# Reordering the head and the second layer norm's lead-in of a fused attention and MLP training kernel

## The chip, the cores and the metric

The kernel runs on one core of a Trainium2 chip. The metric is the device time of one execution in microseconds (us). The core has TensorE (PE, matmuls; PEld are its weight loads), VectorE (DVE), ScalarE (ACT) and GpSimd (POOL). Each of them runs its own instructions in the order in which the program lists them, and waits where one of them needs another engine's result. DMA transfers are issued by SyncE (SP) and POOL, and at some places by ACT. An issue that has to wait holds everything that is queued behind it on the same engine.

## The reference, cut to what matters

```python
h  = x + A(layernorm(x))            # x: 2048 x 640, bf16
#   A: q, k, v = x @ wqkv, 32 heads of 20
#      pq, pk = phi(q), phi(k);  phi(t) = where(t > 0, t + 1, exp(t)) + 1e-6
#      kv = pk^T v per head, z = sum of pk;  o = (pq kv) / (pq z + 1e-6);  A = o @ wo
h2 = h + B(layernorm(h))
#   B: (silu(x @ w1) * (x @ w3)) @ w2,  F = 1728
# outputs: h2 and the gradients for x, wqkv, wo, w1, w3, w2, given grad_out
```

## The kernel before, in words

The 2048 rows are 16 tiles of 128 (`t`), the 640 features 5 chunks of 128. The program is one straight list of instructions, written out by hand; nothing reorders it. `m_part` and its like accumulate in PSUM, for which a few named pairs of buffers ("big", "tr", "m", "mm", "at", "o2") are reused in turn.

**The head (lines 415 to 496).** The x tiles and the key weights (`load_wq(2, 3)` and `(3, 4)`, the two halves) are loaded first, then w2 and grad_out by transposing DMAs. While x tile 0 travels, TensorE runs 44 matmuls on ones. Each tile is normalized by `ln1`: `part` takes the statistics (L147, L150, L151) on VectorE, POOL raises the variance to the power -0.5 (L152), and `norm` subtracts the mean and multiplies (L155). The first eight tiles are transposed on TensorE (`p1_tr`, L249) and copied to `pqT` by ScalarE (L251); the others are transposed by DMA. Step `t` of the loop at L463 then holds, in this order: the key product of tile t in two halves of 320 columns (L255), for t < 3 the transposes of tile t + 1, the statistics of tile t + 4 and the norm of tile t + 3, `phi` (ScalarE's Exp and Relu, L272 and L273, and later VectorE's `rest`, L276 and L277), in some steps a q tile, for steps 2 to 5 a chunk of gradient @ w2^T (`ghh_chunk`, L364 with PSUM "gp") and the transposes of tile t + 2, and from step 3 on the products of pk and normalized x (`m_part`, L385, PSUM "macc"), which read tile t - 3. `trickle` names the steps that load pieces of w1, w3, the v weights and wo.

**After the loop (L498 to L558).** q tiles 4 to 9, the sums `Z` of pk (`z_late`) and their copy over all partitions (`z_row`, L322, L324), the denominators of the attention (`r_prod` on POOL, `r_red`, `r_inv`, `r_scale` on VectorE; `r_head` is the last three and a transposing DMA) and the first two blocks of `kvT` run beside the products of `m_part`. `mT` holds their transposes, by DMA for parts 0 to 3 (L397).

**Lead-in to the MLP (L780 to L790).** The list in `run` names the steps one by one: q tiles 10 to 15 (`q_late`, two halves each), `f2_kv` 2 to 4 (L404, and the masks on VectorE, L205, into `bd`), `f2_wT` 0 to 4 (L610, with a copy and a transposing DMA into `Wp`, L613, L614), then for tiles 0 to 4 the attention's output added to x (`f2_half`, L572, L577), the second layer norm (`f2_hn`) and its transposes (`f2_ht`, L663), with chunks 4 to 7 of gradient @ w2^T (`mlp_ghh`) between them.

**The MLP (L830 to L873).** Four blocks `c` of 512 rows, each with 14 chunks `fc` of F; the last chunk has 64 columns of w2 that are real and 64 of zeros. Chunks come in pairs. For each pair VectorE runs seven operations (`mlp_pair`, L727), three of them with a store to DRAM: `hh` from SP, `gate * gh` from SP and `gh` from POOL. ScalarE writes the next `gate` but one into the same buffer (L693). The second layer norm of the next block's tiles runs beside it.

Of the kernel before, what the change touches and what calls it, by code (L numbers as in the profile page):

```python
# [55 lines left out]
def kernel(  # L56
# [73 lines left out]
    class Stats:  # L130
# [12 lines left out]

        def part(self, src, t, j):
            if j == 0:
                self.st[t] = cp.tile([P, 2, 6], F32, name="st6", bufs=4)
            V.bn_stats(out=self.st[t][:, j, :], in_=src[:, t, j * HD:(j + 1) * HD])  # L147
            if j == 0:
                return
            V.bn_aggr(out=self.mv[:, t, :], in_=self.st.pop(t)[:])  # L150
            V.tensor_scalar(out=self.ve[:, t:t + 1], in0=self.mv[:, t, 1:2], scalar1=EPS_LN, scalar2=None, op0=ALU.add)  # L151
            G.tensor_tensor(out=self.rs[:, t:t + 1], in0=self.ve[:, t:t + 1], in1=mhalf[:, 0:1], op=ALU.pow)  # L152

        def norm(self, out, src, t):
# [24 lines left out]
    def load_x(a, b):  # L179
        dma(out=x_sb[:, a:b, :], in_=xS[:, a:b, :])  # L180

    load_x(1, 2)
    A.activation(sg[:], zero[:], AF.Exp)
    load_wq(2, 3)
    load_wq(3, 4)
    load_x(2, 3)
    load_x(3, 4)
# [44 lines left out]
    XT_DMA = 8  # L232
    WARM = 44

# [9 lines left out]
    def p1_tr(t, parts=((0, DT),)):  # L244
        xn = x_sb[:, t, :]
        for a, b in parts:
# [4 lines left out]
            A.copy(out=pqT[:, a:b, t * P:(t + 1) * P], in_=tr[:, a:b, :])  # L251

    def p1_half(acc, t, n0):
        for c in range(DT):
            T.matmul(acc, lhsT=pqT[:, c, t * P:(t + 1) * P], rhs=wqkv[:, c, n0:n0 + HD], start=(c == 0),  # L255
                     stop=(c == DT - 1))

    def p1_mm(t, n0):
        acc = ps.tile([P, 2, 512], F32, name="big", bufs=2)
        for j in range(2):  # L260
            p1_half(acc[:, j, 0:HD], t, n0 + j * HD)
        return acc

# [4 lines left out]

    def phi(acc, dst, then=None):

        mq, rq = (p1.tile([P, D], BF16, name=n, bufs=b) for n, b in (("mq", 3), ("rq", 3)))
        A.activation(two(mq[:]), acc[:, :, 0:HD], AF.Exp)  # L272
        A.activation(two(rq[:]), acc[:, :, 0:HD], AF.Relu)  # L273

        def rest():
            V.tensor_scalar(out=mq[:], in0=mq[:], scalar1=1.0, scalar2=1e-6, op0=ALU.min, op1=ALU.add)  # L276
            V.tensor_tensor(out=dst, in0=mq[:], in1=rq[:], op=ALU.add)  # L277
            if then is not None:
                then()
        held.append(rest)  # L280
# [18 lines left out]
    def q_tile(t):  # L299
        q_home(t)  # L300
        phi(p1_mm(t, 0), pqs[t])

# [65 lines left out]
    def ghh_chunk(n, acc):  # L368

        c, fc = divmod(n, FT)  # L370
        mm5_to(acc, w2T, fc, g2T[c])
        if n % 2 == 0:
            ghh[n // 2] = pf.tile([P, 2, W], BF16, name="ghh", bufs=4)
        A.copy(out=ghh[n // 2][:, n % 2, :], in_=acc[:])  # L374
# [41 lines left out]
    load_w2T(0, 2 * P)  # L416
    load_g2T(0)
    load_w2T(2 * P, 4 * P)
    load_x(8, 12)
    load_wq(0, 2)  # L420
    load_x(12, ST)
    warm = ps.tile([P, 512], F32, name="warm", tag="tr", bufs=2)
    for _ in range(WARM):
        T.matmul(warm[:, 0:P], lhsT=ones[:], rhs=ones[:], start=True, stop=True, skip_group_check=True)
    ln1.run(x_sb, 0, 1)
    ln1.part(x_sb, 1, 0)
    for a, b in ((0, 2 * P), (2 * P, D)):
        ln1.norm(x_sb[:, 0, a:b], x_sb[:, 0, a:b], 0)
    p1_tr(0, ((0, 2), (2, DT)))
    for t in (1, 2):  # L430
        if t == 1:
            ln1.part(x_sb, t, 1)
            p1_norm(t)
            ln1.run(x_sb, t + 1, t + 2)
        else:
            ln1.part(x_sb, t + 1, 0)
            p1_norm(t)
    ln1.part(x_sb, 3, 1)
    w13 = [go for c0, c1 in ((0, 2), (2, 4), (4, 5)) for go in load_w13(c0, c1)]
    w13 += [lambda: dma(out=w1[:, :, F:FP], in_=rows(B_w3)[:, :, F - FL:F])]  # L440

    def load_wo():
        dma(out=wo[:], in_=A_wo.rearrange("(c p) n -> p c n", p=P))

    trickle = {3: w13[0], 4: w13[1], 11: lambda: load_wq(4, 6), 12: w13[2], 14: w13[3], 15: load_wo}

    stat_of = {t: (t + 4,) for t in range(7)}
    stat_of.update({7: (11, 12), 8: (13,), 9: (14,), 10: (15,)})
    norm_of = {t: (t + 3,) for t in range(8)}
    norm_of.update({8: (11, 12), 9: (13,), 10: (14,), 11: (15,)})  # L450
# [8 lines left out]

    outs = {6: ((group_out, 0),), 7: ((xn_out, 0, dma),), 10: ((group_out, 1), (xn_out, 1, dma)), 13: ((group_out, 2),)}  # L460

    QT = (5, 7, 9, 11)
    for t in range(ST):  # L463
        k = p1_mm(t, D)
        if t < 3:
            p1_tr(t + 1, ((0, 2), (2, DT)))
        for n in stat_of.get(t, ()):
            ln1.run(x_sb, n, n + 1)
            if on_act(n):
                ln1.bias(n)  # L470
        for n in norm_of.get(t, ()):
            if not on_act(n):
                p1_norm(n)
        phi_rest(t < 4)
        phi(k, pk_all[:, t, :])
        for n in norm_of.get(t, ()):
            if on_act(n):
                p1_norm(n)
        if t in QT:
            q_tile(QT.index(t))  # L480
        if 2 <= t < 6:
            ghh_chunk(t - 2, ps.tile([P, 2, 512], F32, name="gp", tag="big", bufs=2)[:, 0])
            p1_tr(t + 2)
        if t >= 3:
# [6 lines left out]
        for f, *n in outs.get(t, ()):  # L491
            f(*n)
        if t in trickle:
            trickle[t]()
    phi_rest()
# [16 lines left out]
    m_end(1)  # L512
    for go in w13[4:]:
        go()
    z_late((2, 3, 4), big())
    m_part(2, range(8))
    z_row((0, 1), big())
    z_row((2, 3, 4), big())
    r_prod(0)
# [4 lines left out]
    r_head(0)  # L524
    load_w2T(4 * P, 8 * P)
    r_prod(2)
# [24 lines left out]
    q_tile(9)  # L551
    r_head(5)
    r_prod(7)
    phi_rest()
# [166 lines left out]
    def mlp_pair(c, k, sig, s2, gate, up, gh):  # L721
# [13 lines left out]
        op(s2, gate, s2)  # L735
        op(gate, gate, gh, to=gg_d, r0=F)
        op(s2, s2, sig, ALU.add)
# [38 lines left out]
    def run(*steps):  # L776
# [4 lines left out]
    pkx.append(p1.tile([P, DT + 6, D], BF16, name="pkx", tag="pk"))  # L781
    run((q_late, 10, f2_mT), (f2_kv, 2), (f2_kv, 3), (f2_kv, 4), (phi_rest,), (q_late, 11), (f2_wT, 0), (f2_wT, 1),
        (phi_rest,), (q_late, 12), (f2_wT, 2), (f2_wT, 3), (phi_rest,), (q_late, 13, lambda: f2_wT(4)),
        (r_red, 6), (r_inv, 6), (r_scale, 6), (load_x, 2, 4), (r_T, 6), (q_late, 14), (load_x, 4, 8), (load_g2T, 1), (r_store, 4, 6),
        (mlp_ghh, 4), (q_late, 15),
        (sig_table,), (f2_half, 0, 0), (f2_half, 1, 0), (f2_half, 0, 1), (f2_half, 1, 1), (f2_hn, 0), (mlp_ghh, 5),
        (f2_half, 2, 0), (f2_hn, 1), (f2_m_out,), (load_w2T, 8 * P, 10 * P), (f2_half, 2, 1),
        (f2_ht, 0), (mlp_ghh, 6), (f2_half, 3, 0), (f2_hn, 2), (f2_w_out,), (f2_ht, 1), (f2_half, 3, 1), (phi_rest, 2),
        (q_out, 10, 14), (f2_ht, 2), (f2_hn, 3), (mlp_ghh, 7), (load_w2T, 10 * P, F), (f2_half, 4, 0), (f2_ht, 3),
        (f2_half, 4, 1), (r4_out,), (r_red, 7), (r_inv, 7), (r_scale, 7), (r_T, 7), (r_store, 6, 8), (q_out, 8, 10))  # L790
    p1.release()
# [38 lines left out]
    for c in range(SC):  # L830
# [8 lines left out]
        for fc in range(FT):  # L839
# [15 lines left out]
            if c == 2 and fc == 3:  # L855
                dmaG(out=rows(kvT_d), in_=bd[:])
            if fc == 3 and 0 < c < SC - 1:
                load_g2T(c + 1)
# [565 lines left out]
```

## Time and profile before

| what | value |
|---|---|
| median of 10 runs | 832.96 us (830.97 to 835.29) |
| profiled execution, own time | 833.86 us |
| its span | 832.2 us |
| VectorE, ScalarE, POOL busy | 454.1, 319.8, 110.5 us |
| granted TensorE clock | 1.00 |
| head and loop | 0 to 54 us |
| after the loop, lead-in to the MLP | 54 to 104 us |
| MLP | 104 to 350 us |

The span runs from the first to the last instruction of one execution; its own time holds what lies around that too. The profile gives, for each instruction, its engine, line, operation, the tile that it writes and those that it reads (`out<-in`), its shape, its start and its length. Idle time of an engine is put down to what ended it. Ends of matmuls are modelled with the pipeline's depth, so gaps between matmuls are better read from their starts. Some matmul records are missing from the trace, about one every ten microseconds.

### The profile page before, as it was taken

How to read it: one execution, taken by the hardware profiler on the slowest of the kernel's cores; microseconds unless marked ns; L12 is line 12 of the kernel's file. 1: busy time of each engine (PE TensorE's matmuls, PEld its weight loads, DVE VectorE, ACT ScalarE, POOL GpSimd, SP SyncE). 2: the span in 40 equal slices, each digit the busy share in tenths (PEclk: the TensorE clock that was granted, in tenths of full speed). 3: DMA queues.
4: the chain of work that ended last, by engine and by line, in shares of the span. 5: the costliest groups of instructions: out<-in, count | busy, mean ns of one | idle time of the engine just before them, and what ended most of it. 6: DMA issues, size and time to landing. Idle time of an engine off the chain costs nothing.

```text
span 832.2 us, 14209 instructions
## 1 busy us (share of the span) xinstructions
PE 818.8 (98%) x5540; PEld 522.8 (63%) x5568; DVE 454.1 (55%) x960; ACT 319.8 (38%) x605; POOL 110.5 (13%) x160
## 2 busy tenths in 40 slices
PE   8999999999999999999999999999999999999998
PEld 5676644555555555777777777777776777555554
DVE  6859787899898656400057777771680445200000
ACT  5855777655555666011121221222211433211111
POOL 2335222122121100000001111110220000000000
PEclk9999999999999999999999999999999999999999
DMA  9799998686574465999767888245998788886771
GB/s 258 206 310 186 215 309 252 219 212 169 143 203 142 129 204 166 211 255 269 218 153 186 185 217 202 62 110 105 237 216 168 172 192 177 212 197 138 164 168 37
DMA packets 323315, 157.59 MB, mean 189 GB/s; under 512 B 235312, under 2 KB 318160, under 8 KB 323248
## 3 DMA queue, kind: packets, MB, share of 16 engines
q1 hardware_dynamic: 293696, 127.73, 64.7%
q0 software_dynamic: 5136, 17.73, 6.5%
q10 hardware_dynamic: 24416, 11.23, 5.9%
q8 instruction: 43, 0.70, 0.4%
q14 instruction: 24, 0.20, 0.1%
HBM read 48.15 MB, written 51.46 MB: 120 GB/s over the span
## 4 chain that ended last, share of the span: by engine, by line
PE 82%; SPq 4%; DMA 1%; ACT 1%; DVE 0%; issue 0%; ACTq 0%
PE mm L364 20%; PE job L1189 17%; PE ghn L991 14%; PE gxn L1348 8%; PE o L751 7%; PE gw L944 7%; PE gwo L1076 3%; PE gr L1048 3%; SPq L1316 2%; PE at L572 2%; SPq L1153 1%; DMA gg_d<-gate 1%; SPq L1099 1%; PE dkv L1292 1%; PE dkv L1221 0%
## 5 line engine op out<-in xcount | busy, mean ns | idle before, releaser
L1189 PE MATMUL job<-gb,hnN 128*128 128x432 bf16 x640 | 117.0, 346 | 0.0
L991 PEld LDWEIGHTS <-ggb 128*128 128x128 bf16 x864 | 84.5, 98 | 32.8
L1189 PEld LDWEIGHTS <-hnN 128*128 128x128 bf16 x640 | 62.6, 98 | 54.1
L364 PE MATMUL mm<-pqT,w 128*128 128x512 bf16 x398 | 93.1, 379 | 0.6
L364 PEld LDWEIGHTS <-w 128*128 128x128 bf16 x540 | 52.8, 98 | 63.4 <-issue 0.3
L1193 ACT CAST obs<-job 128x432 bf16<-128x432 f32 (+1 forms) x60 | 29.2, 487 | 123.1 <-PE job L1189 123.1
L751 PE MATMUL o<-w,hhT 128*128 128x320 bf16 x448 | 67.5, 299 | 0.1
L991 PE MATMUL ghn<-w13a,ggb 128*128 128x320 bf16 x448 | 63.5, 299 | 0.0
L364 PE MATMUL mm<-g2T,w2T 128*128 128x512 bf16 x245 | 62.8, 379 | 0.6
L991 PE MATMUL ghn<-w13b,ggb 128*128 128x320 bf16 x416 | 61.4, 299 | 0.0
L751 PEld LDWEIGHTS <-hhT 128*128 128x128 bf16 x448 | 43.8, 98 | 23.6
L944 PE MATMUL gw<-g,hb 128*128 128x320 bf16 x416 | 57.0, 299 | 0.0
L374 ACT CAST ghh<-mm 128x512 bf16<-128x512 f32 x52 | 30.6, 588 | 55.0 <-PE mm L364 50.0
L944 PEld LDWEIGHTS <-hb 128*128 128x128 bf16 x416 | 40.6, 98 | 15.7
L1348 PE MATMUL gxn<-wqT,gT 128*128 128x320 bf16 x320 | 48.9, 299 | 1.1 <-DMA gT<-g_k 1.0
L1056 POOL TENSOR_TENSOR sz<-Zb,g_h 128x640 f32<-128x640 bf16 x16 | 20.2, 1262 | 199.4 <-DVE g_h L1054 107.7
L691 ACT ACTIVATE sig<-mm 128x512 bf16<-128x512 f32 x56 | 33.6, 599 | 28.3 <-PE mm L364 24.9
L364 PEld LDWEIGHTS <-w2T 128*128 128x128 bf16 x280 | 27.2, 98 | 27.1 <-issue 2.1
L255 PE MATMUL big<-wqkv,pqT 128*128 128x320 bf16 x260 | 39.5, 299 | 2.1 <-ACT pqT L251 0.6
L1003 ACT ACTIVATE gs<-ghn 128x640 bf16<-128x640 f32 x16 | 11.3, 704 | 78.6 <-PE ghn L991 73.7
L255 PEld LDWEIGHTS <-pqT 128*128 128x128 bf16 x320 | 30.6, 97 | 15.5 <-issue 2.2
L1348 PEld LDWEIGHTS <-gT 128*128 128x128 bf16 x320 | 31.1, 98 | 14.0 <-DMA gT<-g_k 1.3
(196 smaller groups left out, 1251.3 us busy)
## 6 DMA issues: line engine op xcount, KB each, us to landing
hh_d<-hhT SPq DMA_DIRECT2D x24, 256.0 KB, 2.6
gg_d<-gate SPq DMA_DIRECT2D x24, 256.0 KB, 3.4
gg_d<-ghh POOLq DMA_DIRECT2D x24, 256.0 KB, 3.4
ggb<-gg_d SPq DMA_DIRECT2D x6, 896.0 KB, 5.7
ggb<-gg_d SPq DMA_DIRECT2D x6, 832.0 KB, 6.1
out_dram<-obs ACTq DMA_DIRECT2D x40, 108.0 KB, 2.7
x_sb<-in_A_x_dram SPq DMA_DIRECT2D x6, 640.0 KB, 6.5
ggb<-gg_d SPq DMA_DIRECT2D x2, 1728.0 KB, 12.5
```

The source lines that it names most:

```text
L255: T.matmul(acc, lhsT=pqT[:, c, t * P:(t + 1) * P], rhs=wqkv[:, c, n0:n0 + HD], start=(c == 0), stop=(c == DT - 1))
L364: T.matmul(acc[:], lhsT=w[:, c, fc * P:(fc + 1) * P], rhs=rhs[:, c, :], start=(c == 0), stop=(c == DT - 1))
L374: A.copy(out=ghh[n // 2][:, n % 2, :], in_=acc[:])
L691: A.activation(sig[:, i, :], gp[:], AF.Sigmoid)
L751: T.matmul(o2["ps"][:, 0:HD], lhsT=hhT[c][:, fc, i * P:(i + 1) * P], rhs=w2[:, fc, j * HD:(j + 1) * HD], start=(fc == 0), stop=(fc == FT - 1))
L944: T.matmul(acc[:, j, 0:HD], lhsT=hb[b][:, t, i * P:(i + 1) * P], rhs=g2[:, t, j * HD:(j + 1) * HD], start=(t == 0), stop=(t == ST - 1))
L991: T.matmul(acc[:, j, 0:HD], lhsT=ggb[t // 2][:, k, lo:lo + P], rhs=rhs[:, j * HD:(j + 1) * HD], start=(k == 0), stop=(k == NG - 1))
L1048: T.matmul(gr[t][:, j, 0:HD], lhsT=ghT[t][:, c, :], rhs=wT2[:, c, j * HD:(j + 1) * HD], start=(c == 0), stop=(c == DT - 1))
L1076: T.matmul(acc[m][:, j, 0:n], lhsT=r_sb[:, t, m * P:(m + 1) * P], rhs=g_hx[:, t, j * HD:j * HD + n], start=(t == 0), stop=(t == ST - 1))
L1189: T.matmul(acc[:, 0:n], lhsT=lhs[:, t, m * P:(m + 1) * P], rhs=rhs(t), start=(t == 0), stop=(t == ST - 1))
L1193: A.copy(out=ob, in_=acc[:, 0:n])
L1348: T.matmul(acc[:, j, 0:HD], lhsT=g, rhs=wqT[:, k, j * HD:(j + 1) * HD], start=(k == 0), stop=(k == 14))
```

## The change

- x tile 2 is loaded between the halves of the key weights, x tiles 8 to 11 ahead of the second part of w2; 36 warm-up matmuls for 44.
- Tile 0 is only centred before it is transposed. Its key and q products get the scale in `phi`; the tile itself is multiplied in step 3 (`p1_scale`), after VectorE's `rest` of that step.
- The transposes of tiles 1 to 7 lie between the two halves of the previous tile's key product, in one piece; the gp chunks move from steps 2 to 5 to steps 3 to 6; the norms of tiles 2 and 3 come ahead of the loop.
- w1 and w3 are loaded in ten pieces and a tail instead of six and a tail, ten of the pieces inside the loop; the v weights are loaded in step 12, the second group of stores moves to step 11, and w2's rows 512 to 1023 are loaded ahead of `z_late`.
- Both `z_row` products use one PSUM buffer.
- `r_head(5)` and `r_prod(7)` move behind the last `f2_wT`; kv blocks and `f2_wT` lie between halves of q tiles; gp chunks 6 and 7 move between the transposes of the second layer norm; some stores and loads of the list move with them.
- The store of `gate * gh` is issued from POOL. The second block of grad_out is loaded in chunk 6 of block 0.
- The last chunk of w2 of each block: its 64 real columns are used twice, each time for 256 of the 512 rows, into PSUM partitions 0 to 63 and 64 to 127; POOL fills the rest of `gh` with zeros.

```diff
         def part(self, src, t, j, mid=None):
...
             V.bn_aggr(out=self.mv[:, t, :], in_=self.st.pop(t)[:])
+            if mid is not None:
+                mid()
...
+        def center(self, out, src, t):
+            V.tensor_scalar(out=out, in0=src, scalar1=self.mv[:, t, 0:1], scalar2=None, op0=ALU.subtract)
...
     load_wq(2, 3)
+    load_x(2, 3)
     load_wq(3, 4)
-    load_x(2, 3)
...
-    WARM = 44
+    WARM = 36
+    RAW = 1
...
+    def p1_scale(t):
+        xn = x_sb[:, t, :]
+        V.tensor_scalar(out=xn, in0=xn, scalar1=ln1.rs[:, t:t + 1], scalar2=None, op0=ALU.mult)
...
-    def p1_mm(t, n0):
+    def p1_mm(t, n0, between=None):
         acc = ps.tile([P, 2, 512], F32, name="big", bufs=2)
         for j in range(2):
             p1_half(acc[:, j, 0:HD], t, n0 + j * HD)
+            if j == 0 and between is not None:
+                between()
...
+        kw = dict(scale=ln1.rs[:, t:t + 1]) if t < RAW else {}
+        A.activation(two(mq[:]), acc[:, :, 0:HD], AF.Exp, **kw)
+        A.activation(two(rq[:]), acc[:, :, 0:HD], AF.Relu, **kw)
...
+        if fc == FT - 1:
+            gh, hw = ghh[n // 2], W // 2
+            G.memset(gh[FL:, 1, :], 0.0)
+            for d in range(DT):
+                for h in range(2):
+                    T.matmul(acc[h * FL:(h + 1) * FL, 0:hw], lhsT=w2T[:, d, fc * P:fc * P + FL],
+                             rhs=g2T[c][:, d, h * hw:(h + 1) * hw], start=(d == 0), stop=(d == DT - 1))
+            for h in range(2):
+                A.copy(out=gh[:FL, 1, h * hw:(h + 1) * hw], in_=acc[h * FL:(h + 1) * FL, 0:hw])
+            return
...
+    load_x(8, 12)
     load_w2T(2 * P, 4 * P)
-    load_x(8, 12)
...
+    ln1.part(x_sb, 0, 0)
+    ln1.part(x_sb, 0, 1, lambda: (center(0, 0, 2 * P), center(0, 2 * P, D)))
+    p1_tr(0, ((0, 2), (2, DT)))
     ln1.part(x_sb, 1, 0)
...
     for t in (1, 2):
+        ln1.part(x_sb, t, 1)
+        ln1.part(x_sb, t + 1, 0)
+        p1_norm(t)
     ln1.part(x_sb, 3, 1)
+    p1_norm(3)
+    w13 = [go for c in range(DT) for go in load_w13(c, c + 1)]
...
+    trickle = {3: w13[0:2], 4: w13[2:4], 9: w13[4:5], 10: w13[5:7], 12: (w13[7], load_vw), 14: w13[8:10], 15: (load_wo,)}
...
-        k = p1_mm(t, D)
-        if t < 3:
-            p1_tr(t + 1, ((0, 2), (2, DT)))
+        k = p1_mm(t, D, (lambda: p1_tr(t + 1)) if t + 1 < XT_DMA else None)
...
         phi_rest(t < 4)
+        if t == 3:
+            p1_scale(0)
...
-        if 2 <= t < 6:
-            ghh_chunk(t - 2, ps.tile([P, 2, 512], F32, name="gp", tag="big", bufs=2)[:, 0])
-            p1_tr(t + 2)
+        if 3 <= t < 7:
+            ghh_chunk(t - 3, ps.tile([P, 2, 512], F32, name="gp", tag="big", bufs=2)[:, 0])
...
-    for go in w13[4:]:
-        go()
+    w13[10]()
+    load_w2T(4 * P, 8 * P)
     z_late((2, 3, 4), big())
     m_part(2, range(8))
-    z_row((0, 1), big())
-    z_row((2, 3, 4), big())
+    zr = ps.tile([P, 2, 512], F32, name="bigx", tag="big", bufs=2)
+    z_row((0, 1), zr[:, 0])
+    z_row((2, 3, 4), zr[:, 1])
...
-    r_head(5)
-    r_prod(7)
...
-        op(gate, gate, gh, to=gg_d, r0=F)
+        op(gate, gate, gh, to=gg_d, r0=F, q=dmaG)
...
+    run((q_late, 10, f2_mT), (q_late, 11, kv3), (phi_rest,), (r_store, 4, 5),
+        (q_late, 12, lambda: (f2_wT(0), f2_wT(1))), (q_late, 13, lambda: (f2_wT(2), f2_wT(3))), (phi_rest,),
+        (q_late, 14, lambda: f2_wT(4)), (load_x, 2, 4), (r_head, 5), (r_prod, 7), (r_red, 6), (r_inv, 6), (f2_m_out,), (f2_w_out,),
+        (load_x, 4, 8), (q_out, 10, 14), (r_store, 5, 6), (load_w2T, 8 * P, 10 * P), (mlp_ghh, 4), (q_late, 15),
...
+        (f2_half, 2, 0), (f2_hn, 1), (load_w2T, 10 * P, F), (f2_half, 2, 1),
+        (f2_ht, 0), (f2_half, 3, 0), (f2_hn, 2), (f2_half, 3, 1), (mlp_ghh, 6), (f2_ht, 1), (mlp_ghh, 7), (f2_ht, 2),
+        (f2_hn, 3), (f2_half, 4, 0), (f2_ht, 3), (f2_half, 4, 1), (r_scale, 6), (r_T, 6), (r_red, 7), (r_inv, 7),
+        (r_scale, 7), (r_T, 7), (r4_out,), (r_store, 6, 8), (q_out, 8, 10))
...
-            if fc == 3 and 0 < c < SC - 1:
+            if fc == (6, 3, 3)[min(c, 2)] and c < SC - 1:
                 load_g2T(c + 1)
```

## The prediction

> **What bounds the kernel now.** I read the page's busy line first, then the waits of TensorE, then a table of stages, then the timeline where the change works.
>
> ```profile
> PE 818.8 (98%) x5540; PEld 522.8 (63%) x5568; DVE 454.1 (55%) x960; ACT 319.8 (38%) x605; POOL 110.5 (13%) x160
> ```
>
> TensorE (PE) is busy 98% of 832.2 us, so a gain needs either fewer PE columns or PE idle time, of which all together is 13.4 us. Where it is, by what ended it (total, times, longest), for 0 to 130 us:
>
> ```profile
> PE gp L364 <- ACT mq L272: 1.3, 1, 1.3
> ...
> PE kv L404 <- DMA mT<-mbs: 0.7, 1, 0.7
> PE wt L610 <- DVE bd L205: 0.6, 1, 0.6
> PE big L255 <- ACT pqT L251: 0.6, 2, 0.3
> PE big L255 <- ACT rq L273: 0.5, 1, 0.5
> ...
> PE big L255 <- ACT Zb L324: 0.3, 1, 0.3
> ```
>
> By stage (busy us of the stretch's length):
>
> ```profile
> 12.00:15.00 3.00, 1.65 (x13) 0.87 (x12) 2.87 (x10) 2.55 (x6) 1.36 (x2) 1.00 1.09 219
> ...
> 31.00:39.00 8.00, 7.28 (x52) 4.86 (x51) 7.31 (x25) 6.63 (x11) 2.86 (x6) 1.00 0.90 227
> ...
> 78.00:92.00 14.00, 12.65 (x116) 9.33 (x116) 11.08 (x29) 11.64 (x32) 2.62 (x4) 1.00 0.70 133
> 92.00:105.00 13.00, 12.36 (x88) 7.45 (x88) 11.05 (x30) 7.84 (x14) 4.57 (x7) 1.00 1.00 253
> ```
>
> The columns after the length: PE, PEld, VectorE (DVE), ScalarE (ACT), POOL, then the granted clock, full throughout. A busy PE hides its pipeline, so I took gaps from the starts of matmuls instead: 512 columns start 216 ns apart (3.24 us for 15 in the chain of waits), 320 columns 136 ns (52.16 us for 384). So measured, PE loses about 5.5 us from 4.9 to 38 us (the head), 0.46 at 58.4, 3.0 from 78 to 105 us, almost nothing in the MLP (105 to 331 us).
>
> **The head: a loss of 1.4 us.** Centring without the scale drops 0.15 us (L151) and 0.57 us (POOL, L152) ahead of the first transposes: 5.50 becomes about 4.65. Worth nothing by itself: the first key weights land at 6.31 us, and the first product already starts at 6.35. Eight warm-up matmuls of 56 ns fall into that cover too. Loading x tile 2 ahead of the second weight half delays that half by one tile, 0.44 us (tiles 2 and 3 landed 7.92 and 8.34), to about 7.9; between the halves lie tile 1's transposes (5 x 56 ns), which wait for its norm at about 7.7. So tile 0's products end near 8.7 instead of 8.2. From there each tile saves its wait for the copy (0.46, 0.46 us at 8.4 and 10.7), and the 1.46 us before the first gp product (g2T landed 14.46) fill with tile 3's work. Up to 16.4 us PE is then about 1 us ahead.
>
> But tile 0 must be scaled before the first macc product reads it, and that multiply is queued on VectorE in step 3, behind tile 7's statistics, tile 6's norm (17.93, 0.44 us) and pk tile 1:
>
> ```profile
> 16.70 0.88 DVE L147 BATCH_NORM_STATS2 st<-x_sb 128x6 f32<-128x320 bf16 x2
> ...
> 18.66 0.44 PE L385 MATMUL macc<-x_sb,pk_all 128*128 128x320 bf16 x2
> ...
> 18.70 0.49 DVE L277 TENSOR_TENSOR pk_all<-mq,rq 128x640 bf16<-128x640 bf16 x1
> ```
>
> VectorE runs nearly without a pause from 3 to 19 us and gets no shorter, so pk tile 1 still ends at 19.2 and the multiply (a norm, 0.44 us) at about 19.55. PE, at this macc at 18.66 today, waits for it from 16.4 to 19.55, with the products of tile 4 queued behind. It has then done one gp product (5 x 216 ns = 1.08 us) and one set of transposes (0.28) less than today: 0.89 + 1.36 = 2.25 us behind. Tiles 4 to 6 also lose the transposes as cover for the PSUM pair "big": after a tile's products PE has 1.08 + 0.28 us of other work, ScalarE needs 0.15 + 0.70 + 0.60 for exp and relu: about 0.15 to 0.2 us each, 0.5. Given back: PE's waits on ScalarE and VectorE at 24.5 to 37 us (0.28 + 0.29 + 0.69 + 0.24 = 1.5 us), of which about 1.35, since VectorE no longer stands 1.78 us for tile 8. Sum: -2.25 - 0.5 + 1.35 = -1.4. Ends: -2.8 if nothing is given back, +1.4 if VectorE is early enough. More is excluded: tile 8's transpose queues behind the first w1/w3 pieces, as many bytes as today (landed 29.18), so its product can't come before 29.8, today 31.17.
>
> **Loads and queues: 0.** q's weights still have the same bytes ahead (23.1 us) and are asked for later than today's 23.3. The small pieces put 1.3 MB into 35 to 45 us, where the DMA share is low; pqT of tiles 13 to 15 passes them with 0.6 us or more to spare, and the stores moved to tile 11 make room. w2T's rows 4P to 8P hold SP 3.1 us, now ahead of mT 2 instead of pqT 1; mT 2 is next needed over 3 us after its landing. The second g2T (SP held 5.18 us) moves from before the MLP into block 0; behind it are hh stores and transposes for block 1. If that cover is gone, up to 1 us.
>
> **z_row: +0.45 us.** One PSUM buffer for both rows leaves the next q tile the buffer of z_late, read long before: the 0.46 us at 58.4 goes (0 to +0.46).
>
> **kv and w blocks, LN 2: +1.9 us.** Today PE stands 0.82 us for mT 3 (landed 79.77), 0.81 + 0.12 for bd, then 0.24 + 0.53 + 0.20 + 0.27 for Wp and LN 2: 3.0 us. With kv after half of q 11 (0.68 us) and mT 3 issued about 2 us earlier, since w2T no longer stands ahead of it, the first wait goes. For bd, r_head 5 is moved out of the way:
>
> ```profile
> 79.03 0.87 DVE L343 TENSOR_REDUCE rden<-pr 128x16 f32<-128x320 f32 x2
> ...
> 80.84 0.97 DVE L350 TENSOR_TENSOR pql<-pql,rden 128x640 bf16<-128x640 bf16 x1
> ...
> 82.56 0.74 DVE L205 TENSOR_TENSOR bd<-kv,mask 128x160 bf16<-128x160 f32 x3
> ...
> 92.13 0.49 DVE L577 TENSOR_TENSOR x_sb<-at,x_sb 128x320 bf16<-128x320 f32 x1 [2.31 <-PE at L572]
> ```
>
> The masks then end near 81.4, before PE asks at 81.9: 1.75 us gained. But r_head 5 (2.3 to 2.7 us) comes back behind the last w copy, with 2.31 us of VectorE idle to take it, less r_scale 6 (0.82, moved behind). LN 2 of four tiles is 8.8 us of VectorE, so its first transpose waits 0.3 to 1.0 us; the two gp products between the others cover the rest. 3.0 - 0.3 to 1.0, less up to 0.4 for the fifth Wp block, which SP can't issue closer than 1.3 us behind the fourth: 1.9 (ends 0.8 and 2.7).
>
> **w2 tail: +1.1 us.** Four chunks of 5 x 216 ns = 1.08 us become ten matmuls of 256 columns and 64 rows. No row shows two column tiles side by side. The nearest has 64 weight columns:
>
> ```profile
> 404.16 2.34 PE L944 MATMUL gw<-g,hb 128*128 128x320 bf16 x16
> ...
> 406.42 0.47 PE L932 MATMUL gttr<-ident,gts 128*64 128x128 bf16 x5
> ...
> 406.82 2.35 PE L944 MATMUL gw<-g,hb 128*128 128x320 bf16 x16
> ```
>
> These start 56 ns apart, as with 128 columns, with 0.09 us lost going in and out. In turn the ten cost 10 x 0.109 + 0.19 = 1.28 us, 0.8 us lost over four. The Trainium skill, "TensorEngine Tiling (Array Packing)", sections Key Properties and Restrictions, speaks for and against: tiles run in parallel, but a change of mode drains the engine and column tiles lose the fast weight load. The drain is the 0.19; slower weights don't show in this row. Side by side, my estimate is 109 ns for 256 columns (from 216 for 512 and 136 for 320) and 6 for the second's start: 5 x 0.115 + 0.19 = 0.77 us, 0.31 x 4 = +1.2. I take +1.1, ends -0.8 and +1.3. The extra POOL memset and second ScalarE copy lie in idle time (ScalarE waits 48.7 us for PE ahead of these copies).
>
> **Gate store on POOL's queue: 0.** 24 full and 8 half stores go from SP to POOL, 0.73 us of issue each for 0.40.
>
> ```profile
> gg_d<-gate SPq DMA_DIRECT2D x24, 256.0 KB, 3.4
> gg_d<-ghh POOLq DMA_DIRECT2D x24, 256.0 KB, 3.4
> ```
>
> Waiting on POOL behind them: LN 2's power, at 12 tiles, for which VectorE waits. ScalarE's next gate copy needs the store landed: today it has 0.1 to 2.9 us left in the first seven pairs and waited once (1.5 us). The Trainium skill, "SBUF — State Buffer", section SBUF: two separate sides, warns that POOL can't write descriptors while VectorE holds the shared port, 620 ns becoming 3100. The row says 3.4 us on either queue beside the same VectorE work; by the rule, my estimate is 2.5 us later. I go with the row: 0 (ends -5 and +0.3).
>
> **Sum.** -1.4 + 0.45 + 1.9 + 1.1 = 2.05 us faster. The profiled execution took 833.86 (span 832.2 and 1.66 around it), so 831.8; the median of ten is 832.96, 0.9 less, so 830.9. Differences under 0.2%, 1.7 us, can't be told from none: faster is below 831.3.
>
> **Rivals.** (A, 45%) as summed: 830.9, between 829.7 and 832.3. (B, 27%) the head's wait is given back, VectorE reaching the multiply by 17.8 us, the bare sum of its work: head +0.9 instead of -1.4: 828.6. For: VectorE's pauses before 12 us. Against: three of them wait for POOL's power and for x 2, as today. (C, 14%) the column tiles run in turn and LN 2 takes 0.8: 832.96 - (-1.4 + 0.45 + 0.8 - 0.8) = 833.9; the change then doesn't do what it says in the MLP. (D, 14%, slower) gate stores land later on POOL's queue. It decides from about 1 us: at +2.5 us pairs 0, 1, 3, 4 and 5 overrun what they have left by 7.1 us in all, some 5 after the 2.1 us that ScalarE waits for PE there anyway: 835.9. For: the rule above; against: the row.
>
> **Range and chances.** 828.0 to 834.4 leaves out D's worst half and the tail of B. Faster: A 0.28 + B 0.26 + C 0.02 = 0.56; same: A 0.17 + B 0.01 + C 0.09 = 0.27; slower: C 0.03 + D 0.14 = 0.17.
>
> **What would show it.** Head: PE idle just ahead of the first macc L385, ended by the new multiply, at about 19.5; B if that wait is under 1 us. z_row: no wait on Zb. kv: no waits on mT or bd, VectorE without a pause before the first L577. Tail: pairs of 64-column matmuls starting a few ns apart; in turn, they stand 109 ns apart. D: ScalarE's gate copy waiting on gg_d. I am wrong if PE clock falls in a longer idle (the longest today is 1.46 us), or if a moved load is late.

## The result and the profile after

The changed kernel takes 836.42 us (median of 14, 834.38 to 841.84); the kernel before, measured again beside it, 831.75 (median of 49). The ratio is 1.0061, 95% interval 1.0047 to 1.0075: slower by about 5 us where the forecast was 830.9. The profiled execution took 837.31 us, its span is 835.6. A stretch of 3.4 us at half clock lowers an execution's mean granted TensorE clock to 0.998, so I count the executions at 0.998 or less: 10 of 14 with the change, 13 of the 167 of the kernel before that were run beside the experiments. The changed kernel's ten have a median of 837.9, its other four of 835.3: the lower clock is a part of the loss, not all of it.

The busy line of the changed kernel:

```profile
PE 818.9 (98%) x5552; PEld 523.5 (63%) x5580; DVE 455.4 (55%) x961; ACT 319.6 (38%) x606; POOL 134.2 (16%) x196
```

TensorE's busy time is the same to 0.1 us, so by this line the 3.4 us of longer span are idle time. The line hides that a matmul at half clock counts as busy for longer. The waits of TensorE in the first 130 us (total, times, longest):

```profile
PE macc L406 <- DVE x_sb L261: 2.9, 1, 2.9
PE at L595 <- DMA Wp<-pkx: 1.9, 1, 1.9
PE big L265 <- DMA wqkv<-in_A_wqkv_dram: 1.2, 1, 1.2
...
PE bigx L333 <- ACT Zb L335: 0.5, 1, 0.5
```

The old waits on mT, bd and mq are gone, as meant. Two of 2.9 and 1.9 us stand in their place: the first macc product waits for tile 0's multiply, and the attention's output waits for a block of Wp. The stages, in the same columns as before (the number behind POOL is the granted clock):

```profile
16.52:19.93 3.41, 0.55 (x3) 0.15 (x2) 3.13 (x11) 1.78 (x3) 0.95 (x2) 1.00 1.06 290
19.93:23.34 3.41, 3.36 (x16) 2.15 (x16) 3.13 (x10) 0.69 (x1) 0.68 (x1) 0.50 1.06 376
31.00:39.00 8.00, 7.85 (x55) 5.12 (x53) 6.12 (x20) 6.87 (x12) 2.26 (x5) 1.00 0.21 43
78.00:92.00 14.00, 13.95 (x130) 10.59 (x129) 11.75 (x30) 11.15 (x31) 2.84 (x4) 1.00 0.71 125
92.00:105.00 13.00, 10.85 (x77) 6.88 (x77) 11.26 (x31) 7.17 (x16) 6.06 (x9) 1.00 0.93 235
```

The second row is what the prediction did not price: behind the long wait TensorE has the clock at half for 3.41 us. From 78 to 92 us it stands still no more (13.95 of 14.00 us; 12.65 before), from 92 to 105 us it stands longer (10.85; 12.36 before). The work in these stretches is not quite the same, since it comes some 4 us later now.

Set against the trace of before, the same matmul comes later by 3.85 us at the end of the loop, 4.02 at q tile 10, 3.69 at the start of the MLP, 3.79 at its end, 3.45 at the end of the span. So the head loses nearly all, and the new lead-in, which was to bring back 1.9 us, brings 0.33. It had brought 1.8 at the first product of the attention's output (93.50 us, 91.25 before); the wait for Wp took that away.

### The profile page after: what moved, and what is told of

The parts are those of the page before. It is cut to its first block, busy times and chain, and to the rows that moved or that the text cites. A ratio compares the mean times of both kernels' runs of the same rounds, so it can differ in the third digit from the quotient of the medians.

```text
span 835.6 us, 14257 instructions
## 1 busy us (share of the span) xinstructions
PE 818.9 (98%) x5552; PEld 523.5 (63%) x5580; DVE 455.4 (55%) x961; ACT 319.6 (38%) x606; POOL 134.2 (16%) x196
## 4 chain that ended last, share of the span: by engine, by line
PE 86%; DMA 5%; DVE 4%; ACT 2%; SPq 1%; issue 1%; POOL 0%; DVEq 0%; ACTq 0%; POOLq 0%
PE job L1216 18%; PE mm L375 18%; PE ghn L1018 14%; PE gw L971 7%; PE gxn L1375 6%; PE o L774 6%; PE big L265 3%; PE gwo L1103 3%; PE gr L1075 3%; PE macc L406 3%; PE dkv L1319 2%; DMA x_sb<-in_A_x_dram 2%; PE at L595 2%; DMA small<-m_d 1%; DVE st L147 1%
## 5 line engine op out<-in xcount | busy, mean ns | idle before, releaser
L375 PE MATMUL mm<-g2T,w2T 128*128 128x512 bf16 x227 | 58.8, 379 | 0.9 <-ACT gate L716 0.2
L395 ACT CAST ghh<-mm 128x512 bf16<-128x512 f32 x48 | 28.2, 588 | 47.9 <-PE mm L375 42.4
L265 PE MATMUL big<-wqkv,pqT 128*128 128x320 bf16 x260 | 41.2, 305 | 1.8 <-DMA wqkv<-in_A_wqkv_dram 1.2
L1030 ACT ACTIVATE gs<-ghn 128x640 bf16<-128x640 f32 x16 | 11.2, 703 | 79.0 <-PE ghn L1018 79.0
L375 PEld LDWEIGHTS <-w2T 128*128 128x128 bf16 x260 | 25.4, 98 | 24.1 <-issue 0.8
```

The costliest lines, as they stand in the source:

```text
L375: T.matmul(acc[:], lhsT=w[:, c, fc * P:(fc + 1) * P], rhs=rhs[:, c, :], start=(c == 0), stop=(c == DT - 1))
```

## The experiments

Each was run in five rounds beside the kernel before; the ratio is to that, with its 95% interval. The kernel before took 831.5 to 832.4 us beside them, so the ratios compare better than the medians.

| kernel | median us | ratio | clock 0.998 or less |
|---|---|---|---|
| changed | 836.42 | 1.0061 (1.0047 to 1.0075) | 10 of 14 |
| scale early | 834.44 | 1.0023 (1.0002 to 1.0044) | 9 of 22 |
| filler | 839.50 | 1.0087 (1.0059 to 1.0115) | 5 of 6 |
| column tiles alone | 831.21 | 1.0000 (0.9982 to 1.0018) | 3 of 14 |
| all but the head | 831.41 | 0.9993 (0.9982 to 1.0004) | 3 of 22 |
| stores late | 841.00 | 1.0083 (1.0057 to 1.0110) | 9 of 11 |
| start filler | 833.98 | 1.0024 (1.0010 to 1.0038) | 16 of 22 |
| gate on SP | 833.82 | 1.0017 (1.0001 to 1.0032) | 13 of 22 |
| h buffers | 828.25 | 0.9963 (0.9949 to 0.9977) | 0 of 6 |
| head alone | 834.87 | 1.0038 (1.0025 to 1.0051) | 3 of 5 |
| lead-in alone | 829.10 | 0.9969 (0.9957 to 0.9981) | 0 of 5 |
| h buffers, gate on SP | 829.10 | 0.9970 (0.9958 to 0.9982) | 0 of 5 |
| the same, z_row as before | 829.04 | 0.9967 (0.9954 to 0.9979) | 0 of 8 |
| large pieces | 836.29 | 1.0062 (1.0036 to 1.0089) | 3 of 10 |
| wo pieces | 832.11 | 0.9999 (0.9985 to 1.0013) | 3 of 12 |
| lead filler | 834.16 | 1.0034 (1.0022 to 1.0047) | 2 of 12 |
| repaired | 833.15 | 1.0023 (1.0012 to 1.0033) | 1 of 11 |
| repaired, five pieces | 830.00 | 0.9975 (0.9966 to 0.9984) | 1 of 10 |
| changed, five pieces | 834.76 | 1.0040 (1.0021 to 1.0060) | 11 of 11 |

### The parts: where are the 5 us?

**Scale early.**

```diff
-        if t == 3:
+        if t == 2:
             p1_scale(0)
```

> The changed kernel with the multiply of tile 0 at the end of step 2 instead of step 3, ahead of tile 7's statistics. Theory H (the loss sits in the head: TensorE waited 2.9 us for that multiply, and ran the 3.4 us behind it at half clock, some 1.6 us): the wait shrinks to about 0.8 us (tile 0 scaled and pk tile 0 ready at 17.5 us instead of 19.9), no half clock, and the time falls by 2.1 + 1.6 = 3.7 us at most against the changed kernel, to about 833; at least by 2.5, if some of it is given back as other waits. Rival V (VectorE as a whole bounds the head up to 25 us, so its order does not matter): pk tile 1 comes 0.4 us later, the waits come back at the next macc, and the time stays at 836 within 0.8. Rival S (the loss is elsewhere: stores of the gate on POOL's queue): 836 too.

The wait is 0.5 us, no stretch has half clock, and the trace stands at the end of the loop where that of before stands (-0.13 us instead of +3.85). In the medians it gains 2.0 us, in the ratio 3.2, of the 5 lost. VectorE does the same work in both orders, so rival V is out: the order was the loss.

**All but the head**: the kernel before's head and loop with its `w13` list, the rest as changed.

> The changed kernel with the kernel before's head (x and weight loads, norm of tile 0, transposes, order of steps 0 to 15 and the large pieces of w1 and w3), all else as changed. Theory H: the head's 3.85 us go, and the other parts are worth -0.4 us together (from 62 us to the end the traces differ by 0.4): 831.4 within 0.5. Rival S (most of the loss comes from the rest, and the head only moves it): 834 or more.

831.41: as theory H has it. **Head alone**: the opposite, the kernel before with the changed head.

> The kernel before with the changed head and nothing else of the change (loads, centring, transposes inside the products, the multiply of tile 0 in step 3, small pieces of w1 and w3). Theory H (the head is the loss, the rest is a small gain): 5.0 us slower than the kernel before, as the changed kernel (836.4) is against all but the head (831.4): 836.5. Rival (the head's lateness is lost again in the lead-in's old waits, which are for transfers): under 833.5.

+0.38%, 3.2 us, not 5: the profiled execution had the 2.9 us wait with no half clock behind it. Head (+3.2) and the rest (-0.6) don't add up to +5.1. The 2.5 us between (by the three intervals, 0.7 to 4.3) are a loss that neither half has by itself. The wait for Wp is one such loss: neither half's trace has it, see below.

**Lead-in alone**: the kernel before with the changed `run` list, `load_w2T(4 * P, 8 * P)` ahead of `z_late`, `r_head(5)` moved, and the second g2T in block 0; against the kernel before, with its other parts:

```diff
+    load_w2T(4 * P, 8 * P)
     z_late((2, 3, 4), big())
...
-    load_w2T(4 * P, 8 * P)
...
-    r_head(5)
-    r_prod(7)
...
-            if fc == 3 and 0 < c < SC - 1:
+            if fc == (6, 3, 3)[min(c, 2)] and c < SC - 1:
```

> The kernel before with only the changed order around the kv and w blocks and LN 2 (w2T's rows 4P to 8P earlier, kv blocks between the halves of q, r_head 5 and the stores of m and w moved, the second g2T in block 0). Theory L (the waits on mT, bd and Wp go, 1.9 us; in the trace of all but the head none of them is left): 830.0 against 831.65. Rival M (what is gained there is lost at the MLP's first pairs, where the moved stores and hn loads now lie): 831.5 within 0.4.

-0.31%, 2.6 us: more than I had predicted for it, and no wait for Wp is left in its trace. In the whole change this gain is lost. **Column tiles alone**: only the new branch of `ghh_chunk`.

> The kernel before with the four w2 tail chunks as column tiles and nothing else of the change. Theory: 0.31 us saved in each, 1.2 us in all: 830.6 against 831.75. Rival (ScalarE's two copies or POOL's fill of the rest come late and give it back): 831.8 or more.

Unchanged within 0.18%; the ratio does not settle a gain of 1.2 us. The trace does: one chunk in the changed kernel,

```profile
141.25 1.24 PE L375 MATMUL mm<-pqT,w 128*128 128x512 bf16 x4
142.42 0.74 PE L387 MATMUL mm<-g2T,w2T 128*64 128x256 bf16 x10
143.09 1.47 PE L375 MATMUL mm<-pqT,w 128*128 128x512 bf16 x6
```

The chunk takes 142.42 to 143.09, 0.67 us, the 0.09 us lost behind it included, and 0.09 us more is lost ahead of it: 0.76 for 1.08. The second matmul of each pair starts 3 to 4 ns after the first. That is 0.32 us saved in each chunk; 0.31 was the estimate. A part of it is taken back at the end of the MLP: TensorE waits there for an output tile's sum, 0.4 us with the column tiles alone, 1.2 with all but the head:

```profile
PE o L760 <- DVE h L765: 1.2, 1, 1.2
```

That sum waits for the store of the tile two before. **H buffers** tests it, on all but the head:

```diff
+    def h_last():
+        return ew("sig")[:].rearrange("p i w -> p (i w)")[:, 0:D]
...
-                    o2["sb"] = pf.tile([P, D], BF16, name="h2", bufs=2)
+                    o2["sb"] = pf.tile([P, D], BF16, name="h2", bufs=2)[:] if c < SC - 1 or i < 2 else h_last()
```

> All but the head, with the last two output tiles of the MLP in buffers of their own instead of the two that rotate. There TensorE stood 1.4 us at 341 us: the sum of the next output tile waited for the store of the tile two before. Theory: the stall goes and 1.0 to 1.4 us with it: 830.2 against 831.4. Rival (the next stage waits for the transposed hh anyway, so the stall only moves behind the last output): 831.4 within 0.3.

The wait is gone from the trace, and the ratio falls from 0.9993 to 0.9963. That is 2.5 us, twice the wait, and the two traces do not show it: their spans are 828.1 and 828.5 us. The profiled execution without the wait was the slowest of its six, that with it 1.6 us below its median. So the gain stands in the medians, and its size is not explained. With 828.25 us this is the fastest kernel here.

### The half clock

**Filler.**

```diff
+        if t == 3:
+            fl = ps.tile([P, 512], F32, name="fill", tag="tr", bufs=2)
+            for _ in range(46):
+                T.matmul(fl[:, 0:P], lhsT=ones[:], rhs=ones[:], start=True, stop=True, skip_group_check=True)
         if t >= 3:
             m_part(0, [t - 3])
```

> The changed kernel with 46 matmuls of ones (128 columns, 56 ns each, 2.6 us; their result is read by nobody) ahead of the first macc product of step 3, where TensorE stood still. The wait for the multiply stays, only TensorE is busy in it. Theory H, clock part: TensorE runs at full clock behind the wait, the first products of tile 4 start 136 ns apart instead of 267, and the time falls by 1.6 us, to about 834.8. Rival (the wait alone costs what is lost, the half clock was hidden by VectorE's work): no change, 836.4 within 0.5.

The mechanism holds, the time does not. From the first gp product to the start of `z_late` TensorE takes 41.10 us instead of 42.78, 1.7 less, with the multiply as late as before (the macc product starts at 19.83, 19.98 in the changed kernel). But this execution lost the clock at two other places, one of them behind a wait of 4.1 us for Wp. Its stages there:

```profile
93.08:96.49 3.41, 1.11 (x9) 0.58 (x6) 2.76 (x8) 1.36 (x2) 1.76 (x3) 1.00 0.94 265
96.49:99.91 3.42, 1.59 (x7) 0.90 (x8) 0.00 (x0) 0.03 (x1) 0.00 (x0) 0.50 1.01 301
99.91:103.32 3.41, 3.41 (x11) 1.51 (x10) 2.07 (x7) 0.82 (x2) 0.94 (x2) 0.50 1.08 263
103.32:106.73 3.41, 3.41 (x29) 2.53 (x28) 2.39 (x7) 1.61 (x3) 0.52 (x2) 1.00 1.09 273
```

The clock changes on a grid of 3.41 us, which lies elsewhere in each execution. A stretch with little work is followed by one at half clock. I took the work of a stretch from the starts and columns of its matmuls (512 columns as 216 ns). In the 20 traces, ten stretches at full clock hold 0.36 of their length or less, and each of them is followed by half clock: 0.11 from 16.5 us in the changed kernel, 0.27 and 0.36 from 93.1 and 4.4 us in this one. All others hold 0.38 or more (0.38 from 825.6 us in repaired, 0.39 from 95.0 us in the changed kernel), and none of them is. The Trainium skill, "TensorE: Matmul & The Clock Gate", Part 1, gives the free-running window of 3413 ns, and has the clock fall after an idle window; here a third of work in it was not enough. So a wait of 2 to 3 us costs 1.7 us more or nothing, by where the grid lies: in head alone the 2.9 us are split over two stretches of 0.48 and more, and cost nothing further. That is one reason why the executions of one kernel differ.

**Start filler.**

```diff
     p1_tr(0, ((0, 2), (2, DT)))
+    fl = ps.tile([P, 512], F32, name="fill", tag="m", bufs=2)
+    for _ in range(16):
+        T.matmul(fl[:, 0:P], lhsT=ones[:], rhs=ones[:], start=True, stop=True, skip_group_check=True)
```

> Scale early, with 16 matmuls of ones (0.9 us) behind tile 0's transposes, where TensorE waits for the first key weights; they end before these land. Theory G (the clock is granted by stretches of 3.41 us, and a stretch in which TensorE is less than about 0.37 busy is followed by one at half clock; the eight warm-up matmuls that were taken out and the earlier transposes leave the first stretches that empty in some executions): executions with a mean clock of 0.998 or less become rare (at most 2 in 10; scale early had 9 of 22, the kernel before 4 of 51), and the median falls by 0.5 to 0.8, to that of scale early's full-clock executions, 833.8. Rival (they come from the wait for the fifth Wp block, 1.8 us): as many as in scale early, 834.4.

Theory G as I put it falls: 16 of 22 executions have a lower clock. In the profiled one it is half from 95.1 to 98.5 us, behind a wait of 3.1 us for Wp, as the rival has it. That count can't see the start, though. The record of the clock begins where it is first full, and ahead of that the warm-up matmuls start 107 ns apart, not 56. In the changed kernel that holds for all of them:

```profile
1.12 4.02 PE L445 MATMUL warm<-ones 128*128 128x128 bf16 x36 [1.12 <-DVE zero L124]
```

In the eight traces with the old head the clock is full from 3.9 to 6.6 us on. Of the twelve with the new one, the two with five pieces have it at half until 9.9 and 10.1 us, and filler has it at half again from 7.8 to 11.2 us. **Lead filler**, on scale early:

```diff
+    def lead_fill():
+        fl = ps.tile([P, 512], F32, name="mm", bufs=4)
+        for _ in range(30):
+            T.matmul(fl[:, 0:P], lhsT=ones[:], rhs=ones[:], start=True, stop=True, skip_group_check=True)
...
-        (sig_table,), (f2_half, 0, 0), (f2_half, 1, 0), (f2_half, 0, 1),
+        (sig_table,), (f2_half, 0, 0), (f2_half, 1, 0), (lead_fill,), (f2_half, 0, 1),
```

> Scale early with 30 matmuls of ones (1.7 us) ahead of the LN 2 product that waits 1.8 us for the fifth Wp block. The wait stays, TensorE is busy in it. Theory G2 (that wait, when it gets longer than some 2 us, empties a stretch of 3.41 us and halves the clock of the next, which makes most of the executions at a lower mean clock): such executions fall from 9 of 22 to 2 in 10 or fewer, and the median to that of the full-clock ones, 833.8. Rival (they come from the MLP's first gate copies or elsewhere): as many as before, 834.4.

2 of 12 against 9 of 22: in the direction of theory G2, too few to settle it. The median stays, as does the wait itself, 1.8 us.

### The wait for the fifth Wp block

Scale early still waits 1.8 us for it; all but the head, with the same lead-in, doesn't. **Stores late**, on scale early:

```diff
-        (r_inv, 6), (f2_m_out,), (f2_w_out,),
-        (load_x, 4, 8), (q_out, 10, 14), (r_store, 5, 6), (load_w2T, 8 * P, 10 * P),
+        (r_inv, 6), (load_x, 4, 8), (load_w2T, 8 * P, 10 * P),
...
-        (f2_half, 1, 1), (f2_hn, 0),
+        (f2_half, 1, 1), (f2_m_out,), (f2_w_out,), (q_out, 10, 14), (r_store, 5, 6), (f2_hn, 0),
```

> Scale early (tile 0's multiply at the end of step 2), and the four kinds of stores on POOL's queue behind the last w block (m, wT, pq, r) moved behind the first four LN 2 halves. In scale early TensorE waited 1.8 us for the fifth Wp block, issued at 89.31 and landed 3.6 us later with those stores beside it; the others took 2.6 us. Theory W (the stores lengthen that landing): it lands in 2.6 us, the wait falls from 1.8 to about 0.8, and the time by 1.0 against scale early: 833.4 against 834.4. Rival (SP's spacing of 1.3 us alone sets it, since the wait is for the issue): wait and time unchanged within 0.3.

Theory W holds for the wait and loses on the time:

```profile
PE mm L375 <- ACT gate L716: 4.3, 1, 4.3
PE at L595 <- DMA Wp<-pkx: 0.6, 1, 0.6
```

The fifth block lands in 2.6 us again. But the stores now lie at the MLP's first pairs, and there TensorE waits 4.3 us behind ScalarE's gate copy, and two stretches at half clock follow. That the stores hold up this copy is likely, not shown.

What differs between the two heads there was SP. Its five Wp issues in h buffers, then in scale early and in the changed kernel (start of the first, time to the end of the fifth):

```profile
82.27 6.50 SPq L623 DMA_TRANSPOSE Wp<-pkx  x5
```

```profile
83.36 7.17 SPq L637 DMA_TRANSPOSE Wp<-pkx  x5
```

```profile
87.34 7.19 SPq L637 DMA_TRANSPOSE Wp<-pkx  x5
```

Without a pause the five take 6.50 us, 1.3 us each. In scale early the third comes at 86.41, 1.72 after the second, though VectorE and ScalarE had copied its data by 85.4. In each of the 20 traces one such pause (0.44 to 0.55 us between issues, 0.1 where SP waits for nothing) stands ahead of SP's 52nd to 55th DMA issue, whatever that issue is. Counted over all of SP's recorded instructions, waits included, that issue is always the 80th or 81st. So the pause goes with the place in SP's program, not with the data. A packet of the instruction queue moved 0.5 to 1.8 us behind its end; that SP fetches its program there is argued, not shown. The small w1/w3 pieces are four issues more ahead of Wp. **Wo pieces**, on h buffers, adds four by other means:

```diff
     def load_wo():
-        dma(out=wo[:], in_=A_wo.rearrange("(c p) n -> p c n", p=P))
+        for c in range(DT):
+            dma(out=wo[:, c, :], in_=A_wo[c * P:(c + 1) * P, :])
```

> The kernel with h buffers (old head, no wait for Wp, 828.25) with the load of wo in five pieces: the same bytes at the same place, four issues more on SP's queue. Theory P: the third Wp issue comes 0.4 us late, the fifth 0.7, and TensorE waits 1 to 2 us for the fifth Wp block: 829.5 to 832. Rival T: no wait for Wp, 828.3 to 829 as without.

```profile
PE mm L364 <- ACT up L709: 1.5, 1, 1.5
PE at L582 <- DMA Wp<-pkx: 1.5, 1, 1.5
```

The wait is there with the old head (the pause ahead of the fourth block, not the third), and the ratio goes from 0.9963 to 0.9999, 3.0 us. From 80 to 125 us TensorE's waits in the two traces go from 1.9 to 4.1 us: 1.5 for Wp, 2.6 behind ScalarE's gate and up copies (1.9 without the pieces). **Large pieces**, on scale early:

```diff
-    w13 = [go for c in range(DT) for go in load_w13(c, c + 1)]
+    w13 = [go for c0, c1 in ((0, 2), (2, 4), (4, 5)) for go in load_w13(c0, c1)]
...
-    trickle = {3: w13[0:2], 4: w13[2:4], 9: w13[4:5], 10: w13[5:7], 12: (w13[7], load_vw), 14: w13[8:10], 15: (load_wo,)}
+    trickle = {3: w13[0:1], 4: w13[1:2], 11: (load_vw,), 12: w13[2:3], 14: w13[3:4], 15: (load_wo,)}
...
-    w13[10]()
+    for go in w13[4:]:
+        go()
```

> Scale early with w1 and w3 in the kernel before's seven pieces at its steps, four issues fewer on SP's queue ahead of the Wp transposes. In every trace SP pauses some 0.4 us ahead of its 53rd or 54th issue: with the changed head that is the third Wp block (86.41 after 84.69, issue 1.5 instead of 1.2 us), with the old one an x load behind the fifth. Theory P (the small pieces slide the Wp transposes onto that pause, the fifth then lands 1 us later beside POOL's stores): the five Wp issues stand 1.3 us apart, TensorE's wait of 1.8 us for the fifth falls under 0.3, executions at a lower mean clock become rare (2 in 10 at most), and the time falls by 2 us to 832.4. Rival T (the old head only differs in how far TensorE is against the transfers): wait 1.5 us or more stays, 834.4.

My expectation missed: the pause only moved, to the fifth block (88.89, 1.71 after the fourth), and the wait is 1.4 us. The kernel is slower than scale early, 1.0062 against 1.0023; its trace has 3.8 us of waits behind gate and up copies at the MLP's start, scale early's 0.7. What lengthens them is open. **Repaired** has the same pieces, with own h buffers and the gate stores on SP.

> The whole change with four repairs: tile 0's multiply at the end of step 2, w1 and w3 in large pieces, own buffers for the last output tiles, gate stores on SP's queue. Theory: the changed head is left with 1.3 us of loss against the old one (waits for the norms of tiles 1 and 2 and for the first weights), and the rest gives 2.9 as in all but the head with h buffers: 829.5 to 830.5. Rival T (the Wp wait stays): 832 or more.

Missed for the same reason: 1.5 us of wait, pause ahead of the fifth. **Repaired with five pieces** takes two issues more away:

```diff
-    w13 = [go for c0, c1 in ((0, 2), (2, 4), (4, 5)) for go in load_w13(c0, c1)]
+    w13 = [go for c0, c1 in ((0, 2), (2, 5)) for go in load_w13(c0, c1)]
```

> The repaired kernel with w1 and w3 in five pieces instead of seven (chunks 0-1, 2-4), two issues fewer on SP's queue, same bytes. In the repaired kernel SP's pause of 0.4 us lies ahead of its 52nd issue, the fifth Wp block; now that is the 50th. Theory P: the pause falls behind the five Wp issues, they stand 1.3 us apart, the fifth lands in 2.6 us, TensorE waits under 0.4 us for it instead of 1.5, and the time falls by 1.2 to 2.5: 830.7 to 832. Rival T (the stores of POOL's queue lengthen that landing wherever SP's pause lies): wait 1.3 us or more, 833.2.

```profile
84.16 6.50 SPq L638 DMA_TRANSPOSE Wp<-pkx  x5
```

```profile
PE at L596 <- DMA Wp<-pkx: 0.2, 1, 0.2
```

The five stand 1.3 us apart, the wait is 0.2, and the ratio goes from 1.0023 to 0.9975, 4.0 us (3.2 in the medians). From 80 to 125 us TensorE's waits go from 2.9 to 0.9 us; the two traces do not show where the rest comes from. **Changed with five pieces** is the changed kernel with this edit only.

> The changed kernel with w1 and w3 in these five pieces, nothing else different; the multiply of tile 0 stays in step 3. Theory P: the head's loss stays (wait of 2.9 us), the wait for the fifth Wp block goes from 1.9 to under 0.4, and 1.5 to 3 us with it: 833.5 to 835 against 836.4. Rival T: 836.4 within 0.5.

The wait for Wp is 0.2 us there too and the late multiply costs 2.7 us; 834.76, ratio 1.0040, an interval that overlaps that of the change. All 11 executions have the lower clock, in the profiled one from the head alone. Without the wait for Wp, head and rest add up within the intervals: 0.38% - 0.07% is 0.31%, measured is 0.40%. For the wait, theory P is shown from both sides: four issues more bring it (wo pieces), two or six fewer remove it (here), and four fewer only move the pause to another block (large pieces).

### Gate store and z_row

**Gate on SP**, on scale early:

```diff
-        op(gate, gate, gh, to=gg_d, r0=F, q=dmaG)
+        op(gate, gate, gh, to=gg_d, r0=F)
```

> Scale early with the gate stores back on SP's queue. Theory S (stores on POOL's queue land later, 4.2 us against 3.4, which ScalarE's gate copies and the last output stores feel): the stalls at 118 us (0.9) and at the end of the MLP (1.6 us) shrink together by 1 us or more: 833.4. Rival N (those stalls have other causes: the last output stores wait beside SP's transposes of hh, and they appear with the column tiles alone too, 1.2 and 0.6): unchanged within 0.4, 834.4.

Both stalls are gone from its trace, as theory S has it, but a wait of 1.8 us for a load of x is new, the two medians differ by only 0.6 us and the intervals overlap. **H buffers with gate on SP**, the same edit:

> The kernel with h buffers, and the gate stores back on SP's queue. Theory S (as in gate on SP: ScalarE's gate and up copies wait less): TensorE's waits of 1.0 and 0.9 us behind the gate and up copies near 118 us go, 0.5 to 1.5 us: 827.2 against 828.25. Rival N (those waits come from the moved stores of m, w and q, ahead of any gate store): 828.2 within 0.4.

No gain: 0.9970 against 0.9963. The changed kernel's stores do land later:

```profile
gg_d<-gate POOLq DMA_DIRECT2D x24, 256.0 KB, 4.2
gg_d<-ghh POOLq DMA_DIRECT2D x24, 256.0 KB, 3.6
```

0.8 us later than on SP before (3.4), not the 2.5 that I worked out from the rule on the shared port, and TensorE waits 0.2 us behind a gate copy. **Z_row as before**, on the last one:

```diff
-    zr = ps.tile([P, 2, 512], F32, name="bigx", tag="big", bufs=2)
-    z_row((0, 1), zr[:, 0])
-    z_row((2, 3, 4), zr[:, 1])
+    z_row((0, 1), big())
+    z_row((2, 3, 4), big())
```

> The same as the run before it in this list, with z_row's two PSUM buffers as in the kernel before. Theory Z (sharing one buffer made the second z_row product wait 0.5 us for ScalarE's copy of the first, and saved the next q tile a wait of the same kind, 0.5 us): no difference, within 0.3 us. Rival (sharing is worth the 0.45 us that I predicted): 0.45 slower.

No difference (829.04 and 829.10).

## Why the prediction was wrong

**The head, -1.4 us: the failing step.** The mechanism was right. VectorE's rows of the changed kernel:

```profile
19.14 0.49 DVE L290 TENSOR_TENSOR pk_all<-mq,rq 128x640 bf16<-128x640 bf16 x1
19.55 0.38 DVE L261 TENSOR_SCALAR x_sb<-x_sb,ln_rs 128x640 bf16<-128x640 bf16 x1
```

Three terms of the sum were missing or mis-sized:

- The multiply starts at 19.55, where I had its end, and the macc product at 19.98. So TensorE is 1.32 + 1.36 = 2.7 us behind, not 2.25.
- The half clock behind the wait, 1.7 us, was named as what would make me wrong and priced at nothing, though the wait that I forecast, 3 us, was twice the longest in the trace.
- "Given back 1.35" was 0.93. Even that was there to be had only in the profiled execution of before: in it and one other trace of the old head, a stretch from 33 us on takes 4.46 us; in the other six it takes 3.54. I had taken off 0.9 us from the profiled time to reach the median, and counted the same stall once more as a gain.

With these the sum is -2.7 - 1.7 - 0.5 + 0.93 = -4.0; the trace is 3.85 behind that of before at the end of the loop. Even this is too little, since that trace was a late one: `z_late` starts at 53.3 to 55.1 us in the eight traces with the old head, median 53.55, and at 58.60 in the changed kernel. That is 5.05 us, as much as the whole loss. In head alone, without half clock there, it is 56.49, 2.9 behind, and the time 3.2; the eight with the early multiply have a median of 54.7, so the new head is 1.2 us behind even then.

Two readings at the start were off without deciding anything. 5.50 less 0.15 and 0.57 is 4.78, not 4.65, and the first transposes came at 4.94; and the warm-up matmuls do not stand 56 ns apart before the clock is full.

**Loads and queues, 0: wrong for SP.** I followed bytes and landings of the moved loads, not the count of issues. Four more put SP's pause among the Wp blocks. The trace of before had it, too: its fifth Wp block was issued at 90.25, 1.74 us after the fourth, with no store of POOL's close behind.

**kv and w blocks, LN 2, +1.9: right as a part, lost in the whole.** Alone 2.6. With the change, "up to 0.4 for the fifth Wp block" was 1.9 us: about 0.7 from the pause, and 1.1 from a landing in 3.7 instead of 2.6 us. POOL's first store is issued 0.3 us behind it there; with this lead-in and no pause among the five, that store comes 0.95 us behind, and the block lands in 2.6. Stores late, with the stores moved away, had 2.6 as well.

**z_row, +0.45: moved, not removed.** The second product writes the buffer that ScalarE still copies; it waits 0.5 us there, which the next q tile no longer does.

**w2 tail, +1.1: right in the chunk** (0.32 us each), but from the MLP's first product to its last the changed trace takes 245.1 us, that of before 245.0. The wait for the output tiles' two buffers, 0.8 us, took back a part; I had not asked what is late next there. In the ratio of column tiles alone nothing is left that could be told from none.

**Gate store, 0: right within what the runs can tell.** Rival D came out on the right side, slower, by luck: its reason is not the one.

**Rivals.** A fell by the half clock and Wp, B is out (the wait was 2.9 us, not under 1), C is out (pairs start 3 to 4 ns apart).

What stays open: what SP does in its pause, how much of the loss in single executions is the grid's place (lead filler was too few executions), and what lengthens the waits behind ScalarE's copies at the MLP's start, which go from none (changed with five pieces) to 4.3 us (stores late).

## What to carry to other kernels

Price a wait of TensorE by its length and by the half clock that can follow. From about 2 us on, within one stretch of 3.41, it cost 1.7 us more here; so move the late step, not the wait. A load split into more pieces also changes the place of every later issue on its queue; look there for a step with no slack, and count issues as well as bytes. What is subtracted to get from a profiled execution to the median must not be counted again as a gain of the change; where there are several traces of the kernel before, look first which of its waits are in all of them.

## What I had not expected of the hardware

- SP pauses about 0.4 us at one place of its program, ahead of the 80th or 81st of its recorded instructions, here its 52nd to 55th DMA issue. Four issues more or two fewer shift what is hit. The kernels with and without that differ by 3.0 us (wo pieces) and 4.0 us (repaired, seven or five pieces), of which their traces show some 2 us as waits of TensorE.
- The transposing DMA of the fifth Wp block landed in 2.6 to 2.7 us where no store of POOL's was near, and in 3.4 to 5.6 us where the first of them was issued within 0.7 us of it (nine traces).
- A stretch of 3.41 us at full clock in which TensorE's matmuls filled 0.36 or less was followed by half clock, ten times in 20 traces; one of 0.38 or more never was.
